# Power table stored and mask read back through ScalarE's own queue, first weights issued ahead of the mask

## The chip, the core and the metric

The kernel runs on one core of a Trainium2 chip. The metric is the device time of one execution in microseconds (us), the median of three runs. Engines are named as the profile names them: PE (TensorE), with PEld for its weight loads, DVE (VectorE), ACT (ScalarE), POOL (GpSimd) and SP (SyncE, which in this kernel does nothing but issue transfers).

## The reference: retention, a gated mixture, a feed-forward layer

Only the first of the three stages touches the change. It is a retention layer over 2 batches, 8 heads, 768 positions and 64 features, in blocks:

```
Dmask = np.where(rel >= 0, lam[:, None, None] ** rel[None, :, :], 0.0)
intra = np.einsum('bhic,bhjc->bhij', qb, kb) * Dmask[None]
intra = np.einsum('bhij,bhjd->bhid', intra, vb)
inter = np.einsum('bhid,bhde->bhie', qb * lam_pow[None], kv_state)
out[:, :, sl] = intra + inter
kv_state = lam_block[None, :, None, None] * kv_state + np.einsum('bhsd,bhse->bhde', kb_dec, vb)
```

Its output, 1536 tokens of 512 features, goes through four experts, `out += p[:, e:e + 1] * (relu(x @ w1[e]) @ w2[e])` with normalised gates `p`, and then through `(g @ w_out)` with `g = h * sigmoid(h)` and `h = x @ w_in`. These two stages are nearly all of the matrix work.

## The kernel before

**Tiling.** Retention works on blocks of 128 positions: 6 blocks (c) for each of 2 batches (b) make 12 units, u = 2c + b. A unit has four pieces: `prep` (`qs`, the queries times powers, POOL), `scores` (`ks` on POOL, `s` on PE, then `a` = `s` times `dmask` on DVE), `mix` (`xps` on PE, then its high and low parts `xhi` on ACT and `xlo` on DVE) and `carry` (`sps` on PE, then the state). Every large product is made of three products of a high and a low part. So a weight tile is split before use: ACT rounds it to the high part (`ua` from the raw tile `u`, `dh` from `d`, line 139), and DVE or POOL subtracts to get the low part (`ub`, `dl`, line 140). The raw tiles `u` (line 113) and `d` (line 118) have two buffers each, and the next load into one is issued after the split of the old content.

**Order.** The program fixes the order on each engine by the order in which it is written (a manual schedule). The experts' products (`ph`, line 469, then `po`, line 524) for the first 256 tokens begin once units 0 and 1 are mixed; the rest of the retention is put between them. `keep_warm` issues products on PE whose result nobody reads: three before the first scores, five between the scores and `xps`.

**Powers.** `powers()` loads `lam` (8 numbers), doubles its way to a table of 256 powers per head on DVE (`z`, line 268), stores it to memory (`zd`), and reads it back twice: as the mask `dmask` (two transfers of 256 KB, made of runs of 128 numbers with overlapping addresses) and as the factors `qdec` (two of 128 KB). Each of these, like every other transfer of the kernel before, is issued by SP. SP takes its instructions in order; one that waits holds up those behind it.

**Semaphores of transfers.** The framework gives transfers eight completion semaphores, DMAHW0 to DMAHW7, in turn. A transfer that takes a semaphore again is not issued until the transfer that used it last has landed. So SP also waits for transfers with whose data it has nothing to do. The listings below show these waits in brackets.

**Gates.** After the fourth step of the experts, `gates()` normalises the expert probabilities with nine small operations on DVE (lines 313 to 319, tile `gate`, loaded at line 309).

Of the kernel before, what the change touches and what calls it, by code (L numbers as in the profile page):

```python
# [37 lines left out]
def kernel(  # L38
# [10 lines left out]
    nc = tc.nc  # L49
# [25 lines left out]
    zd = dram.tile([H, 2 * P], F32, name="zd")  # L75
# [20 lines left out]
    def load_qk(c, b):  # L96
        t = ald.tile([P, 2, NPAIR, P], F32, tag="qk", name="qkt")
        nc.sync.dma_start(out=t, in_=qk[c, b])
        qk_t[c, b] = t

    def load_kv(c, b, parts=(slice(0, 2),)):
        if (c, b) not in kv_t:
            kv_t[c, b] = ald.tile([P, 2, H, D], F32, tag="kv", name="kvt")
        for j in parts:
            nc.sync.dma_start(out=kv_t[c, b][:, j], in_=kv[c, b, :, j])
# [25 lines left out]
    def load(j, n=1):  # L131
        for _ in range(n):
            if nxt[j] < len(seq):
                ph, i, src = seq[nxt[j]]
                nxt[j] += 1
                (load_up, load_down)[j](src, i, (ph, i))
# [120 lines left out]
    def powers():  # L257
        z = acst.tile([H, 2 * P], F32, name="z")
        nc.sync.dma_start(out=z[:, P:P + 1], in_=lam)
        nc.vector.memset(z[:, :P - 1], 0.0)  # L260
        nc.vector.memset(z[:, P - 1:P], 1.0)
        for b in range(B):
            load_qk(0, b)
        load_kv(0, 0, [1])
        m = 1
        while m < P:
            o = P - 1 + m
            nc.vector.tensor_scalar_mul(z[:, o + 1:o + 1 + m], z[:, P:o + 1], z[:, o:o + 1])
            m *= 2
        nc.sync.dma_start(out=zd, in_=z)  # L270
        load_kv(0, 1, [1])
        for m in range(2):
            nc.sync.dma_start(
                out=dmask[:, 2 * m:2 * m + 2],
                in_=bass.AP(
                    zd.tensor, zd.offset + m * H * P, [[1, P], [2 * P, NPAIR], [1, P]]
                ),
            )
        load(0)
        for b in range(B):  # L280
            load_kv(0, b, [0])
        for t in range(2):
            nc.sync.dma_start(
                out=qdec[t * D:(t + 1) * D],
                in_=bass.AP(
                    zd.tensor, zd.offset + t * 2 * P + P, [[0, D], [4 * P, NPAIR], [1, P]]
                ),
            )
        for b in range(B):
            nc.gpsimd.memset(state[b], 0.0)  # L290
        keep_warm(3)

    def keep_warm(n):
        warm = psum.tile([P, NPAIR, P], F32, tag="po3", name="warm")
        for _ in range(n):
            nc.tensor.matmul(
                warm, lhsT=state[0][:, 0], rhs=state[0], start=True, stop=True
            )
# [499 lines left out]

    with tc.manual_schedule():
        powers()  # L800
        load(1)
        load(0)
# [232 lines left out]
```

## Time and profile before

| | |
|---|---|
| Median of 3 runs | 828.22 us (827.99 to 828.74) |
| Profiled execution | 826.95 us, of which the span of the trace is 825.2 us |
| PE busy | 811.7 us, 98% of the span |
| DVE, ACT, POOL busy | 535.1, 323.0, 456.6 us |
| Granted TensorE clock | 1.0 of full over the span's 40 slices, by the page |

The profiled execution is 1.27 us below the median of the runs. Times in rows count from the start of the span. A row of a timeline gives start, duration, engine, source line, operation, output and inputs; in brackets stands how long the engine was idle before it and what ended that.

### The profile page before, as it was taken

What the parts mean: (1) busy time and instruction counts of PE and PEld (TensorE: products, weight loads), DVE (VectorE), ACT (ScalarE), POOL (GpSimd) and SP (SyncE); (2) the same over time, 40 slices, a digit from 0 to 9 for tenths busy, and PEclk for the clock granted to TensorE, in tenths of its full rate; (3) what the DMA queues carried; (4) which work ended last, traced back from release to release, by engine and by line L of the source; (5) the groups of instructions that cost most, each with busy time, mean ns of one, the idle gap of its engine ahead of it and who ended that gap; (6) DMA issues with size and microseconds to landing.
All of it is one profiled execution on the core that took longest, in us unless ns stands there. A gap on an engine that the chain in (4) does not pass through costs nothing.

```text
span 825.2 us, 10886 instructions
## 1 busy us (share of the span) xinstructions
PE 811.7 (98%) x4144; PEld 672.4 (81%) x4144; DVE 535.1 (65%) x776; ACT 323.0 (39%) x508; POOL 456.6 (55%) x334
## 2 busy tenths in 40 slices
PE   9899999999999999999999999999999999999998
PEld 5799778888878888888888888888888888888886
DVE  4876957475758577777877777765345345666666
ACT  3424232323346433333333333334445465444431
POOL 1724646353558566666666666654356566656631
PEclk9999999999999999999999999999999999999999
DMA  8885756542333223222322211222333131111002
GB/s 285 321 297 174 260 196 241 186 137 89 128 124 120 90 90 116 89 90 90 115 90 90 90 64 65 64 69 87 100 102 100 55 102 51 52 52 52 25 1 102
DMA packets 31432, 95.92 MB, mean 116 GB/s; under 512 B 3408, under 2 KB 5000, under 8 KB 31380
## 3 DMA queue, kind: packets, MB, share of 16 engines
q1 hardware_dynamic: 31380, 95.23, 34.4%
q8 instruction: 32, 0.52, 0.3%
q14 instruction: 20, 0.16, 0.1%
HBM read 83.65 MB, written 11.57 MB: 115 GB/s over the span
## 4 chain that ended last, share of the span: by engine, by line
PE 90%; DVE 5%; DMA 2%; ACT 1%; issue 1%; SPq 0%; ACTq 0%; DVEq 0%
PE po L706 32%; PE po L524 14%; PE ph L469 13%; PE y L646 12%; PE z L646 8%; PE x L646 8%; DMA d<-wts 2%; PE s L364 1%; PE xps L391 1%; PE xps L382 1%; DVE lo L562 1%; DVE tail L204 1%; DVE dec L207 1%; ACT hhi L496 0%; DVE dec L201 0%
## 5 line engine op out<-in xcount | busy, mean ns | idle before, releaser
L718 DVE TENSOR_TENSOR acc<-po,acc 128x512 f32<-128x512 f32 x176 | 117.2, 683 | 54.4 <-PE po L706 54.3
L706 PE MATMUL po<-hhi,dh 128*128 128x512 f32 x384 | 149.4, 389 | 0.0
L706 PE MATMUL po<-hhi,dl 128*128 128x512 f32 x384 | 149.4, 389 | 0.0
L706 PE MATMUL po<-hlo,dh 128*128 128x512 f32 x384 | 149.4, 389 | 0.0
L140 POOL TENSOR_TENSOR dl<-d,dh 128x1024 fp32r<-128x1024 f32 (+1 forms) x48 | 114.1, 2376 | 27.7 <-ACT dh L139 27.6
L140 POOL TENSOR_TENSOR ub<-u,ua 128x256 fp32r<-128x256 f32 (+2 forms) x48 | 75.5, 1573 | 91.8 <-ACT ua L139 87.5
L663 POOL TENSOR_TENSOR s<-s,s 128x512 f32<-128x512 f32 x48 | 68.5, 1428 | 45.0 <-ACT s L658 44.9
L140 POOL TENSOR_TENSOR uc<-u,uc 128x512 fp32r<-128x512 f32 x24 | 30.9, 1288 | 98.3 <-ACT uc L139 98.3
L706 PEld LDWEIGHTS po<-hhi,dl 128*128 128x128 f32 x384 | 72.1, 188 | 15.1
L706 PEld LDWEIGHTS po<-hlo,dh 128*128 128x128 f32 x384 | 72.1, 188 | 15.0
L706 PEld LDWEIGHTS po<-hhi,dh 128*128 128x128 f32 x384 | 72.1, 188 | 14.9
L496 ACT ACTIVATE hhi<-ph 128x512 fp32r<-128x512 f32 x40 | 24.0, 599 | 111.3 <-DVE ph L490 97.5
L140 POOL TENSOR_TENSOR ub<-us,ua 128x1024 fp32r<-128x1024 f32 x24 | 57.7, 2403 | 5.0 <-ACT ua L139 5.0
L469 PE MATMUL ph<-xhi,ua 128*128 128x512 f32 (+1 forms) x224 | 55.5, 370 | 3.5 <-DVE hlo L480 2.8
L524 PE MATMUL po<-hhi,dh 128*128 128x512 f32 (+1 forms) x224 | 58.7, 364 | 0.1
L524 PE MATMUL po<-hhi,dl 128*128 128x512 f32 (+1 forms) x224 | 57.7, 359 | 0.0
L524 PE MATMUL po<-hlo,dh 128*128 128x512 f32 (+1 forms) x224 | 57.6, 359 | 0.0
L139 ACT ACTIVATE dh<-d 128x1024 fp32r<-128x1024 f32 (+1 forms) x52 | 51.3, 988 | 11.3 <-issue 3.1
L469 PE MATMUL ph<-xhi,ub 128*128 128x512 f32 (+1 forms) x224 | 53.2, 359 | 0.0
L469 PE MATMUL ph<-xlo,ua 128*128 128x512 f32 (+1 forms) x224 | 53.0, 359 | 0.0
L343 POOL TENSOR_TENSOR qs<-qkt,qdec 128x512 f32<-128x512 f32 x10 | 12.9, 1290 | 67.3 <-PE xps L382 52.3
L469 PEld LDWEIGHTS ph<-xhi,ua 128*128 128x128 f32 x224 | 37.8, 188 | 11.8 <-DVE hlo L480 3.2
(127 smaller groups left out, 1600.9 us busy)
## 6 DMA issues: line engine op xcount, KB each, us to landing
u<-wts SPq DMA_DIRECT2D x32, 512.0 KB, 3.5
d<-wts SPq DMA_DIRECT2D x32, 512.0 KB, 4.0
words<-wts SPq DMA_DIRECT2D x32, 512.0 KB, 6.0
wd<-dec SPq DMA_DIRECT2D x32, 256.0 KB, 4.1
u<-wd SPq DMA_DIRECT2D x16, 512.0 KB, 3.7
d<-wd SPq DMA_DIRECT2D x16, 512.0 KB, 3.8
qkt<-qk SPq DMA_DIRECT2D x12, 512.0 KB, 6.2
kvt<-kv SPq DMA_DIRECT2D x10, 512.0 KB, 5.0
```

The lines of the kernel that those rows point to most:

```text
L139: nc.scalar.activation(out=hi, in_=src, func=AF.Copy)
L140: eng.tensor_tensor(out=lo, in0=src, in1=hi.bitcast(F32), op=ALU.subtract)
L204: nc.vector.tensor_scalar(out=tail, in0=low, scalar1=2.0 ** -29, scalar2=None, op0=ALU.mult)
L207: nc.vector.scalar_tensor_tensor(out=f, in0=high, scalar=3, in1=f, op0=ALU.logical_shift_left, op1=ALU.bitwise_or,)
L343: nc.gpsimd.tensor_tensor(out=qs, in0=qkt[:, 0], in1=qdec, op=ALU.mult)
L469: nc.tensor.matmul(pt[:, :n], lhsT=w, rhs=x[:, k, o:o + n], start=(j == 0), stop=(j == len(ops) - 1),)
L496: nc.scalar.activation(out=hi, in_=pt, func=AF.Copy)
L524: nc.tensor.matmul(po_t[d][:, :n], lhsT=w[:, d * P:(d + 1) * P], rhs=h[:, :n], start=(begin and j == 0), stop=(last and j == 2),)
L646: nc.tensor.matmul(to, lhsT=a[:, k * P:(k + 1) * P], rhs=b[:, k], start=(first and j == 0), stop=(j == len(ops) - 1), skip_group_check=not ...
L663: nc.gpsimd.tensor_tensor(out=t, in0=a, in1=b, op=ALU.add)
L706: nc.tensor.matmul(po, lhsT=w, rhs=h, start=(j == 0), stop=(j == len(ops) - 1))
L718: nc.vector.tensor_tensor(out=a, in0=po, in1=a, op=ALU.add)
```

## The change

In `powers()` the store of the table and the four reads of it (two of `dmask`, two of `qdec`) are issued by ACT in place of SP. The first load of up-weights, `load(0)`, is written ahead of the mask reads. Nothing else in the program is altered.

```
-        nc.sync.dma_start(out=zd, in_=z)
+
+        nc.scalar.dma_start(out=zd, in_=z)
         load_kv(0, 1, [1])
+        load(0)
         for m in range(2):
-            nc.sync.dma_start(
+            nc.scalar.dma_start(
                 out=dmask[:, 2 * m:2 * m + 2],
...
-        load(0)
         for b in range(B):
             load_kv(0, b, [0])
         for t in range(2):
-            nc.sync.dma_start(
+            nc.scalar.dma_start(
                 out=qdec[t * D:(t + 1) * D],
```

SP before, from the second half of the first values and keys to the third down-weight load. `zd` is the table in memory, `u` and `d` raw weights, `kvt` keys and values, `qkt` queries and keys; the two rows behind these are the `qkt` loads of block 1.

```order
L270 DMA zd<-z 8x256 [waits DMAHW0_49,DVE_49]
L105 DMA kvt<-kv 128x512
L273 DMA dmask<-zd 128x4x128 [waits DMAHW4_49]
L273 DMA dmask<-zd 128x4x128
L113 DMA u_145<-wts 128x1024
L105 DMA kvt<-kv 128x512 [waits DMAHW1_49]
L105 DMA kvt<-kv 128x512 [waits DMAHW2_49]
L283 DMA qdec<-zd 64x4x128 [waits DMAHW3_49]
L283 DMA qdec<-zd 64x4x128
L118 DMA d_157<-wts 128x1024 [waits DMAHW5_49]
L113 DMA u_159<-wts 128x1024 [waits DMAHW6_49]
L118 DMA d_161<-wts 128x1024 [waits DMAHW7_49]
```

SP after, the same stretch, up to the `qkt` loads of block 1.

```order
L98 DMA qkt<-qk 128x1024 x2
L105 DMA kvt<-kv 128x512 x2
L113 DMA u_143<-wts 128x1024
L105 DMA kvt<-kv 128x512 [waits DMAHW0_49]
L105 DMA kvt<-kv 128x512 [waits DMAHW2_49]
L118 DMA d_157<-wts 128x1024 [waits DMAHW4_49]
L113 DMA u_159<-wts 128x1024 [waits DMAHW6_49]
L118 DMA d_161<-wts 128x1024 [waits DMAHW7_49]
L98 DMA qkt<-qk 128x1024 [waits DMAHW1_49,DMAHW0_49,PE_49]
L98 DMA qkt<-qk 128x1024 [waits DMAHW1_49,PE_49]
```

SP no longer waits for DVE or for the store before the first weights, but semaphores now tie its loads to ACT's transfers: the first `d` takes over DMAHW4 from the store, the second `u` takes DMAHW6 from the first `u`, the second `d` takes DMAHW7 from the first mask read, and the second `qkt` takes DMAHW1 from the second mask read.

ACT before, from its first instruction.

```order
L139 ACT_TABLE_LOAD
L139 ACTIVATE ua<-u_145 128x2x256 [waits DMAHW0_49]
L403 ACTIVATE xhi<-xps 128x4x128 [waits PE_49] x2
L139 ACTIVATE ua<-u_145 128x512
L139 ACTIVATE dh<-d_157 128x512 [waits DMAHW5_49]
```

ACT after, from its first instruction.

```order
L271 DMA zd<-z 8x256 [waits DMAHW0_49,DVE_49]
L275 DMA dmask<-zd 128x4x128 [waits DMAHW4_49]
L275 DMA dmask<-zd 128x4x128 [waits DMAHW1_49]
L284 DMA qdec<-zd 64x4x128 [waits DMAHW3_49]
L284 DMA qdec<-zd 64x4x128 [waits DMAHW5_49]
L139 ACT_TABLE_LOAD
L139 ACTIVATE ua<-u_143 128x2x256 [waits DMAHW6_49]
L404 ACTIVATE xhi<-xps 128x4x128 [waits PE_49] x2
```

The five transfers stand ahead of everything else on ACT, the load of its function table included. On PE, DVE and POOL the order of instructions is the same in both programs.

## Rows read from the trace of the kernel before

**Rows 1.** The page's first part: busy time, share, instructions.

```profile
PE 811.7 (98%) x4144; PEld 672.4 (81%) x4144; DVE 535.1 (65%) x776; ACT 323.0 (39%) x508; POOL 456.6 (55%) x334
```

**Rows 2.** Longest wait of PE in the whole span: total us, times, longest.

```profile
PE ph L469 <- DVE hlo L480: 2.8, 1, 2.8
```

**Rows 3.** Windows: length, busy PE PEld DVE ACT POOL, clock, DMA share, GB/s.

```profile
36.19:38.98 2.79, 0.00 (x1) 0.00 (x1) 2.79 (x5) 0.00 (x0) 2.71 (x4) 1.00 1.01 389
60.00:825.00 765.00, 756.64 (x3659) 626.37 (x3658) 493.93 (x695) 304.13 (x472) 432.76 (x308) 1.00 0.31 102
```

**Rows 4.** The chain that ended last, at 4 us: start, duration, what.

```profile
4.02 2.75 DMA zd<-z
```

**Rows 5.** Timeline of PE, 8 to 16 us.

```profile
8.60 4.56 PE L296 MATMUL warm<-state 128*128 128x512 f32 x10
13.09 1.97 PE L391 MATMUL xps<-a,kvt 128*64 128x128 f32 x32
15.76 0.51 PE L469 MATMUL ph<-xhi,ua 128*128 128x256 f32 x2 [0.70 <-ACT xhi L403]
```

**Rows 6.** Timeline of DVE and ACT, 8 to 16 us.

```profile
10.69 2.78 DVE L372 TENSOR_TENSOR a<-s,dmask 128x256 f32<-128x256 f32 x8 [6.69 <-DMA dmask<-zd]
13.07 0.63 ACT L139 ACTIVATE ua<-u 128x512 fp32r<-128x512 f32 x1 [11.05 <-DMA u<-wts]
15.11 0.60 ACT L403 ACTIVATE xhi<-xps 128x512 fp32r<-128x512 f32 x1 [0.28 <-PE xps L391]
```

**Rows 7.** Windows of the first 30 us, columns as in rows 3.

```profile
4.20:6.20 2.00, 2.00 (x4) 0.51 (x2) 0.00 (x0) 0.00 (x0) 0.00 (x0) 1.00 0.99 394
6.20:7.20 1.00, 1.00 (x11) 0.59 (x12) 0.00 (x0) 0.00 (x0) 0.00 (x0) 1.00 0.54 207
7.20:8.20 1.00, 1.00 (x24) 1.00 (x22) 0.00 (x0) 0.00 (x0) 0.00 (x0) 1.00 0.05 16
8.20:10.20 2.00, 2.00 (x14) 1.14 (x11) 0.00 (x0) 0.00 (x0) 0.00 (x0) 1.00 0.79 223
...
16.20:28.20 12.00, 11.98 (x126) 11.25 (x125) 7.58 (x16) 6.76 (x15) 4.36 (x5) 1.00 1.03 409
```

**Rows 8.** Timeline of PE, PEld, ACT and DVE, 23 to 29 us.

```profile
23.52 0.53 PEld L469 LDWEIGHTS ph<-xhi,ub 128*128 128x128 f32 x4 [0.21 <-DVE ub L140]
24.58 0.63 ACT L139 ACTIVATE ua<-u 128x512 fp32r<-128x512 f32 x1 [2.91 <-DMA u<-wts]
26.11 1.16 PE L364 MATMUL s<-qkt 64*128 64x128 f32 x16
27.27 0.54 PEld L469 LDWEIGHTS ph<-xhi,ua 128*128 128x128 f32 x4 [0.20 <-DVE hlo L480]
28.45 1.28 DVE L372 TENSOR_TENSOR a<-s,dmask 128x512 f32<-128x512 f32 x2
```

**Rows 9.** Tile `gate`, to 46 us: ns min/median/max, first and last start; landing.

```profile
L319 DVE TENSOR_TENSOR gate<-gate x4: 291/1020/1362, 35.1 to 37.9; 12x128 f32<-12x128 f32 x4
L309 SPq DMA_DIRECT2D gate<-probs x1: 390/390/390, 24.5 to 24.5; - x1
...
DMA to landing us min/median/max: 5.2/5.2/5.2
```

**Rows 10.** Timeline of ACT and SP, 0 to 8 us.

```profile
0.73 1.28 ACT L139 ACT_TABLE_LOAD   x1 [0.73 <-PEq L1022]
2.06 0.43 SPq L105 DMA_DIRECT2D kvt<-kv  x1
7.76 0.50 SPq L113 DMA_DIRECT2D u<-wts  x1
```

**Rows 11.** Tile `zd`: issues of its reads, ns; issue to landing of `dmask`.

```profile
L273 SPq DMA_DIRECT2D dmask<-zd x2: 382/445/508, 6.8 to 7.2; - x2
L283 SPq DMA_DIRECT2D qdec<-zd x2: 679/704/728, 9.4 to 10.2; - x2
...
DMA to landing us min/median/max: 3.8/4.0/4.2
```

## The prediction

> **What bounds the kernel now.** I read the busy shares first: PE works 811.7 of 825.2 us [rows 1], so no change of waits can win more than 13.5 us. PE's waits come next: the longest is 2.8 us, for DVE's `hlo`, and ends at 38.98 [rows 2, 3]; the stretch from 60 us on has another 765.0 − 756.6 = 8.4 us without PE work [rows 3], which no transfer of the start reaches directly.
>
> The chain of waits looks as if the start hung on the power table: it names 2.75 us for the store [rows 4], and DVE's first `a` waits 6.69 us for the mask [rows 6]. The reader should not take this for PE's path. PE fills that time with products nobody reads, until 13.16, and they stand ahead of `xps` in its order [rows 5]. So `xps` starts at 13.1 however early its inputs are. It ends at 15.06, the second `xhi` runs from 15.11 to 15.71 [rows 6], and `ph` starts at 15.76 [rows 5]. The first `ua` was done at 13.70 [rows 6]. So **weights that come earlier save nothing at the first `ph`**.
>
> Then the transfers, the full resource of the first 30 us. From 16.2 to 28.2 the DMA engines are busy at share 1.03 with 409 GB/s, but from 7.2 to 8.2 they stand nearly idle (0.05), while the mask waits for the store [rows 7]. What that backlog delays is seen at 24 to 30 us: ACT waits 2.91 us for the third `u`, and its later `hhi` and DVE's `hlo` follow late, so `a` of unit 2 starts at 28.45 [rows 8] and ends at 29.7. The gates come next on DVE, and the probabilities land just then, 24.5 + 5.2 = 29.7 [rows 9]. Nine gate operations stand ahead of the `hlo` for which PE waits at 38.98.
>
> **The change part by part.**
>
> *SP.* It loses a wait: the first `u` is issued at about 2.9 (one `kvt` issue at 2.06 takes 0.43, a second as much) in place of 7.76 [rows 10]. By the new order the first `d` waits only for the store. The second `d` and the second `qkt` wait for the two halves of the mask.
>
> *ACT.* It issues five transfers, by SP's durations 0.38 + 0.51 for the mask, 0.68 + 0.73 for `qdec` and, taken like the shortest of these, 0.38 for the store, 2.7 us [rows 11], waits for the store between, and loads its table behind them, 1.28 us [rows 10]. From 6.2 us, when I put the store's landing: 0.9 for the mask, 1.4 for `qdec`, 1.3 for the table, done at 9.8. I cost it at nothing: ACT has nothing before 13.07 now [rows 6], and PE needs from it the `xhi` behind `xps`. Without that cover it would cost the whole 3.6 us. No row has a transfer issued by ACT; were each issue twice as long, ACT would be free by 12.1.
>
> *The gain, behind the backlog.* Idle shares times lengths, 0.46 × 1 + 0.95 × 1 + 0.21 × 2 = 1.8 us between 6.2 and 10.2 [rows 7], can be filled with weights; and the mask moved at 223 GB/s where large rows moved at 394, so mixed with these it may give back some more. I take 2 us: the third `u`, its `d` and the probabilities land 2 us sooner. Then `a` of unit 2 hangs on PE's scores and no longer on ACT: these start at 26.11 less the PEld stall of 0.21, last 1.16 and end at 27.06, against the start of `a` at 28.45: **1.4 us** [rows 8]. Gates and `hlo` follow by as much. PE arrives 0.4 us sooner (0.21 and 0.20), so its stall of 2.79 shrinks to 1.8, and PE goes on 1.4 us ahead. Bounds: 0 if the stream gains nothing, 2.79 + 0.41 = 3.2 us if the whole stall goes.
>
> *The loss, at the mask.* Now the mask reads are alone in the one queue, ahead of the weights: issued at 6.8 and 7.2, they land 3.8 and 4.2 us later, at 10.6 and 11.4 [rows 11]. The first two of eight `a` start at 10.69; the other six need the second half and take from 11.40 to 13.47, 2.07 us [rows 6]. A quarter of `xps` (0.49) must follow the last `a`. So `xps` ends at T + 2.56, where T is the landing of the second half, and not before 15.06 [rows 5]: **up to T = 12.5 nothing is lost, from there each us late costs PE one**. After the change the mask shares the engines with whatever SP has out. Low bound: it is served at once; the store takes 2.75 us as today at most, T is 11.4 or less, loss 0. High bound: all that SP may have out goes first. From 2.4 to 7.6 us, at 394 GB/s, the queue moves 2 MB: two `qkt`, two `kvt` and `u` (a 128x1024 tile of 4-byte numbers is 512 KB). Left are two `kvt` of 256 KB, `d` and the second `u`, 1.57 MB or 4.0 us. With a store 0.6 us quicker than now, since it no longer stands behind `qkt` and `kvt`, T = 11.4 − 0.6 + 4.0 = 14.8, loss 2.3 us. I take T = 13.6, **loss 1.1 us**, the middle: the mask goes in runs of 512 bytes, `u` in rows of 4 KB, so by turns the mask has the worse of it, but `u` and the second `u` come one after the other.
>
> The Trainium skill (DMA: Bandwidth & Descriptors, "Queues, rings and completion order") says that each DMA engine goes round the queues that have work, a packet of several descriptors at a time. If such packets hold about the same time on both queues, T by that rule would be near 12.8 and the loss 0.3 us, an estimate. No run here has two queues at work yet.
>
> *Sum.* −1.4 + 1.1 = −0.3 us on the profiled 826.95, which lies 1.27 below the median: 826.65 there, **827.9 us** beside the median of 828.22.
>
> **The rivals.**
>
> *The mask is starved* (slower). If SP's second `d`, free once the first mask half has landed, also passes the second half, T rises by another 1.3 us to 16.1, the loss to 3.6, the sum to +2.2: 830.4 us. For it: large rows against short ones, and a second `d` that waits for the first half only. Against: `u`, `d` and the second `u` wait for semaphores and so come in slices. It decides from T = 12.5 + 1.4 + 1.66 = 15.6 on.
>
> *The mask is served at once.* Loss 0, sum −1.4: 826.8 us. For it: the store and mask then have a queue without a backlog. Against: the same 16 engines.
>
> *The whole stall goes* (faster). One gate operation took 291 ns against a median of 1020 [rows 9], while POOL worked through nearly all of the stall (2.71 of 2.79) [rows 3]. If POOL, fed earlier, is through with its splits, nine gates take some 2.6 us and not 9: sum −3.2, 825.0 us. Against: POOL's work follows ACT and PE, and it is busy to the end of the stall.
>
> *No gain from the order of issue.* The stream is full from 10 us on; if its semaphores hold SP up as long as the store did, `u` and probabilities come at today's times: 828.2, or 829.3 with the mask late. The Trainium skill (same page, "Issuing engines are not separate DMA queues") states just this: a second issuing engine saves sequencer time alone. The trace bears it out in part, since the stream runs at share 1.03, but it also shows the idle 2 us.
>
> **How the numbers follow.** Chances: forecast (mask late by 0 to 2.3 us beyond its slack, sum −1.4 to +0.9) 0.50; starved 0.16; served at once 0.17; whole stall 0.09; no gain 0.08. About 0.2% (1.66 us) is what a measurement of this kernel can tell from no change. Forecast and no gain lie within it but for 1 in 20 on either side, since the 8.4 us without PE work after 60 us [rows 3] may shift by about 1 us; so do four fifths of served at once; starved is slower in all but 1 of 10. Together faster 0.15, same 0.67, slower 0.18. The likeliest case spans 826.8 to 829.1; the range reaches to the starved case and below served at once: 826.3 to 830.2.
>
> **What would show it.** Right: the first `u` issued near 3 us; `a` of units 0 and 1 starting later than 10.69, with a gap between its first two and the rest; `xps` ending at 15.1 to 17.4; no wait of ACT for the third `u`; PE's stall at 36 us near 1.8. Wrong: `xps` after 17.4 (starved), DVE's gates much shorter than 9 us (whole stall), ACT still waiting some 2.9 us for the third `u` (no gain), or a change of PE's waits after 60 us larger than that before.

## The result, and the profile after

The changed kernel takes 833.92 us (median of 6 runs, 832.81 to 835.88) beside 828.61 us for the kernel before: ratio 1.006, 95% interval 1.0048 to 1.0072. It is 5.3 us slower, where 827.9 us and no change that can be told were forecast. The profiled execution has 832.96 us with a span of 831.2, 6.0 us more than the span before.

The timeline of the start, after. The lines stand in order of time; those of ACT's queue are marked ACTq, those of SP's SPq.

```profile
3.02 0.52 SPq L113 DMA_DIRECT2D u<-wts  x1
3.58 2.96 SPq L105 DMA_DIRECT2D kvt<-kv  x2
3.87 0.55 ACTq L271 DMA_DIRECT2D zd<-z  x1
7.68 4.56 PE L297 MATMUL warm<-state 128*128 128x512 f32 x10
9.70 0.33 SPq L118 DMA_DIRECT2D d<-wts  x1
9.70 0.99 ACTq L275 DMA_DIRECT2D dmask<-zd  x2
10.11 0.40 SPq L113 DMA_DIRECT2D u<-wts  x1
12.39 1.28 ACT L139 ACT_TABLE_LOAD   x1 [12.39 <-issue]
16.53 0.33 SPq L118 DMA_DIRECT2D d<-wts  x1
16.61 0.76 DVE L373 TENSOR_TENSOR a<-s,dmask 128x256 f32<-128x256 f32 x2 [12.77 <-DMA dmask<-zd]
17.83 2.08 DVE L373 TENSOR_TENSOR a<-s,dmask 128x256 f32<-128x256 f32 x6 [0.46 <-DMA dmask<-zd]
18.35 3.56 PE L392 MATMUL xps<-a,kvt 128*64 128x128 f32 x32 [6.11 <-issue]
22.62 0.73 PE L470 MATMUL ph<-xhi,ua 128*128 128x256 f32 x4 [0.70 <-ACT xhi L404]
...
37.00 0.44 DVE L314 TENSOR_TENSOR gate<-gate 12x128 f32<-12x128 f32 x1 [1.05 <-DMA gate<-probs]
```

What to see, against [rows 4 to 6]: the store is issued at 3.87, a little sooner than before, but the reads of it only at 9.70, where the wait for the store ends; before these were 4.02 and 6.79. The second half of the mask lets `a` go on at 17.83, before at 11.4. PE has emptied its warm products at 12.24 and stands idle for 6.11 us. Then `xps` takes 3.56 us, where it took 1.97. The first `ph` starts 22.62 − 15.76 = 6.86 us later than before.

That the store stood behind SP's transfers is seen in the packets by queue (q1 is SP's, q10 is ACT's and is not there in the kernel before; packets, MB, share of the 16 engines), first from 4.5 to 7.5 us, then from 7.5 to 9.5:

```profile
q1 hardware_dynamic: 431, 1.08, 98.9%
```

```profile
q1 hardware_dynamic: 302, 0.69, 95.7%
q10 hardware_dynamic: 16, 0.01, 1.4%
```

ACT had issued the store by 4.42, but no packet of it moved before 7.5 us, while SP's filled the engines.

Why `xps` is slower stands in the windows (columns as in [rows 3]; the three numbers at the end are the granted clock, the DMA share and GB/s).

```profile
10.00:11.00 1.00, 1.00 (x4) 0.50 (x3) 0.00 (x0) 0.00 (x0) 0.00 (x0) 1.00 0.27 68
...
14.00:15.00 1.00, 0.00 (x0) 0.00 (x0) 0.00 (x0) 0.31 (x1) 0.00 (x0) 0.92 1.04 406
15.00:16.00 1.00, 0.00 (x0) 0.00 (x0) 0.00 (x0) 0.00 (x0) 0.00 (x0) 0.50 1.07 347
...
20.00:21.00 1.00, 1.00 (x14) 1.00 (x12) 0.55 (x1) 0.60 (x1) 0.01 (x1) 0.50 0.90 315
21.00:22.00 1.00, 0.92 (x10) 0.63 (x6) 0.69 (x1) 0.03 (x1) 0.00 (x0) 0.67 0.88 352
```

PE idles from 12.24; late in the window from 14 to 15 the granted clock drops from 1.00 to 0.50, the lower level of 1.2 GHz, and stays there through `xps`, until after 21. The DMA engines are busy meanwhile, at a share of 1.04 and 1.07: the mask waits its turn. They were not from 10 to 11 us: SP's `d` waits for the store's landing too, so the stream ran low (0.27) just when the mask reads were issued.

The wait of PE that answers to [rows 2], after:

```profile
PE ph L470 <- DVE hlo L481: 1.6, 1, 1.6
```

The stall behind the gates has shrunk from 2.8 to 1.6 us, so part of the forecast gain is there: of the 6.86 us lost at the first `ph`, some 0.8 us come back by the end of that stall, and the span ends 6.0 us longer.

### The profile page after: what moved, and what is told of

It reads as the page before. It is cut to its first block, busy times and chain, and to the rows that moved or that the text cites. A ratio compares the mean times of both kernels' runs of the same rounds, so it can differ in the third digit from the quotient of the medians.

```text
span 831.2 us, 10886 instructions
## 1 busy us (share of the span) xinstructions
PE 812.2 (98%) x4144; PEld 673.9 (81%) x4144; DVE 533.8 (64%) x776; ACT 323.2 (39%) x508; POOL 456.8 (55%) x334
## 4 chain that ended last, share of the span: by engine, by line
PE 91%; DVE 5%; issue 1%; DMA 1%; ACT 1%; POOL 0%; SPq 0%; ACTq 0%; DVEq 0%; POOLq 0%
PE po L707 31%; PE po L525 14%; PE ph L470 13%; PE y L647 12%; PE z L647 8%; PE x L647 8%; PE xps L392 1%; PE s L365 1%; PE warm L297 1%; PE xps L383 1%; DMA wd<-dec 1%; DVE lo L563 1%; DMA gate<-probs 1%; DVE tail L204 1%; DVE dec L207 1%
```

## The experiments

Eight kernels were run. The theory that took shape from the trace above: **a queue of its own gives the store and the mask no precedence; they come behind whatever SP has issued before or beside them, and SP, no longer waiting, now issues more.** The first rival: it is the weights written ahead of the mask. The second: transfers issued by ACT are slow in themselves. Ratios are to the kernel before on the same chip, with the 95% interval.

### The two halves of the change, each alone

First, the weights ahead, all transfers with SP: the store, and likewise the four reads of mask and decays.

```
-        nc.scalar.dma_start(out=zd, in_=z)
+        nc.sync.dma_start(out=zd, in_=z)
...
         load_kv(0, 1, [1])
         load(0)
```

> Half of the change alone: all transfers stay with SP, only the first weight load is written ahead of the mask reads. Theory 'the own queue gives no precedence' (what SP issued ahead of the store and the mask is moved first, wherever they are queued): the store keeps its place behind 1.25 MB and lands near 6.8 us, the mask reads stand behind one more 512 KB load, so the second half lands near 12.0 to 12.7 and xps ends at 15.1 to 15.4; the transfers have no idle stretch at 7.2 to 8.2 us, so PE's stall at 36 us shrinks by about 1 us: 827.0 to 828.2 us, nothing lost. Rival 'weights ahead of the mask are what costs': the mask half lands after 15 us and most of the 5 us loss of the changed kernel is here.

Measured: 827.68 us, ratio 0.9987 (0.9977 to 0.9997), a gain of about 1 us. Its timeline:

```profile
6.65 0.93 SPq L275 DMA_DIRECT2D dmask<-zd  x2
10.16 0.63 ACT L139 ACTIVATE ua<-u 128x512 fp32r<-128x512 f32 x1 [8.14 <-DMA u<-wts]
11.36 2.87 DVE L373 TENSOR_TENSOR a<-s,dmask 128x256 f32<-128x256 f32 x8 [7.50 <-DMA dmask<-zd]
15.64 0.74 PE L470 MATMUL ph<-xhi,ua 128*128 128x256 f32 x4 [0.70 <-ACT xhi L404]
```

The mask is 0.7 us later than before, within its slack, and the first `ph` is not later at all. The first rival falls. The stall behind the gates is 2.4 us, only 0.4 us less than before, where about 1 us less was expected.

Then the queue alone, for the store and the four reads, with `load(0)` in its old place.

```
-        nc.sync.dma_start(out=zd, in_=z)
+        nc.scalar.dma_start(out=zd, in_=z)
```

> The other half alone: store, mask and qdec issued by ACT, the first weight load written where it was. SP has nothing left to wait for between, so the order on SP and on ACT comes out as in the changed kernel. Theory 'own queue gives no precedence': as the changed kernel, 833 to 835 us, the store landing near 9.7 and the second mask half near 17.8 us. Rival 'weights ahead of the mask are what costs': back near 828.6 us.

Measured: 834.52 us, ratio 1.0071 (1.0056 to 1.0087). Its reads are issued at 9.15 and its `a` goes on at 17.13:

```profile
9.15 0.99 ACTq L273 DMA_DIRECT2D dmask<-zd  x2
17.13 2.08 DVE L372 TENSOR_TENSOR a<-s,dmask 128x256 f32<-128x256 f32 x6 [0.23 <-DMA dmask<-zd]
```

The whole loss comes with ACT's queue; the weights ahead are by themselves a small gain (the run before). This run parts the two less well than it seems: with nothing of `powers()` left on SP, `u` is issued at 3.01 here too, so SP's and ACT's orders are those of the changed kernel.

### The store given back to SP

```
-        nc.scalar.dma_start(out=zd, in_=z)
+        nc.sync.dma_start(out=zd, in_=z)
```

> The changed kernel with the store alone given back to SP, where it stands ahead of the second kvt half, of u and of the other kvt loads. Theory 'own queue gives no precedence': the store lands near 6.8 us, the mask reads on ACT start some 3 us sooner than in the changed kernel but behind u, two kvt and beside d: second half at 13.5 to 15.5 us, xps ends at 16 to 18, 829 to 832 us. Rival 'transfers issued by ACT are slow in themselves': the mask still needs some 8 us from its issue, as in the changed kernel (9.70 to 17.83), so it lands near 15 or later, with few bytes of SP in flight beside it.

Measured: 831.83 us (830.98 to 834.55), ratio 1.0046 (1.0027 to 1.0064), in the theory's range. The profiled execution is the slowest of the five, 834.55. In it the mask came later than the theory's 13.5 to 15.5 us:

```profile
6.62 0.98 ACTq L275 DMA_DIRECT2D dmask<-zd  x2
9.96 0.33 SPq L113 DMA_DIRECT2D u<-wts  x1
16.66 2.08 DVE L373 TENSOR_TENSOR a<-s,dmask 128x256 f32<-128x256 f32 x6 [2.08 <-DMA dmask<-zd]
```

The reads are issued 3.1 us sooner than in the changed kernel, and the second half is in only 1.2 us sooner, 10.0 us after the issue. That fits a mask that waits also for the second `u`, issued 3.3 us behind it; taken alone it would fit the second rival as well. The next run parts them.

### ACT's queue without company

SP's later loads are held until the mask is in, by a store of 4 KB of its second half.

```
         load_kv(0, 1, [1])
-        load(0)
         for m in range(2):
             nc.scalar.dma_start(out=dmask[:, 2 * m:2 * m + 2], ...)
+        hold = dram.tile([8, P], F32, name="hold")
+        nc.sync.dma_start(out=hold, in_=dmask[:8, 3, 1])
+        load(0)
         for b in range(B):
             load_kv(0, b, [0])
```

> ACT issues store, mask and qdec as in the changed kernel, but SP first writes 4 KB of the second mask half back to memory and so issues u, the rest of kvt, d and the second u only once the mask is in. Theory 'the mask waits behind what SP has on the same engines': with only qkt and kvt ahead (1.5 MB) the store lands at 6.5 to 7.3 us and the mask halves 3.7 to 4.8 us after their issue, as when SP issued them, so a starts at 10.5 to 11.5; the weights are then later than before and the total is between the kernel before and the changed one. Rival 'transfers issued by ACT are slow in themselves': the mask halves still need 7 to 8 us from their issue, a starting at 13.5 us or later.

Measured: 833.12 us, ratio 1.0051 (1.0032 to 1.007), from two runs. What was asked of it is in the timeline:

```profile
3.87 0.55 ACTq L271 DMA_DIRECT2D zd<-z  x1
7.60 0.94 ACTq L274 DMA_DIRECT2D dmask<-zd  x2
11.52 0.76 DVE L375 TENSOR_TENSOR a<-s,dmask 128x256 f32<-128x256 f32 x2 [7.69 <-DMA dmask<-zd]
12.56 2.08 DVE L375 TENSOR_TENSOR a<-s,dmask 128x256 f32<-128x256 f32 x6 [0.28 <-DMA dmask<-zd]
...
17.28 0.63 ACT L139 ACTIVATE ua<-u 128x512 fp32r<-128x512 f32 x1 [6.07 <-DMA u<-wts]
18.94 0.76 PE L472 MATMUL ph<-xhi,ua 128*128 128x256 f32 x4 [3.59 <-ACT xhi L406]
```

The same reads, issued by the same engine, land 3.9 and 4.5 us after their issue when SP sends nothing beside them; issued by SP alone they took 3.8 and 4.2 [rows 11]. The second rival falls. The kernel is slower than the one before all the same, since the weights now come 4.2 us later and `ph` starts 3.2 us later, behind them; the clock also falls to 0.50 behind that wait. In these two kernels with two queues either the mask is late or the weights are.

Three kernels give one line. From the issue of the first mask read to the go of the last six `a` it takes 5.0 us with nothing beside it, 8.1 us in the changed kernel, where SP sent `d` and the second `u` (1.05 MB), and 10.0 us with the store on SP, where the first `u`, two `kvt`, `d` and the second `u` were out (2.1 MB). At 400 GB/s these bytes are 2.6 and 5.2 us; added to 5.0 they give 7.6 and 10.2. The store goes the same way: 2.8 us from its issue to the reads' issue with 1.25 MB ahead of it on SP [rows 4], 3.7 in the last run with 1.5 MB ahead, 5.8 in the changed kernel with 2.3 MB. Which of the bytes to count was settled only after these runs had been seen.

### How the two queues take turns: not settled

The mask is read in one transfer in place of two; a small read of `lam` stands in the place of the second.

```
-        for m in range(2):
-            nc.scalar.dma_start(out=dmask[:, 2 * m:2 * m + 2], ...)
+        nc.scalar.dma_start(out=dmask,
+            in_=bass.AP(zd.tensor, zd.offset, [[1, P], [2 * P, H], [1, P]]))
+        nc.scalar.dma_start(out=spare, in_=lam)
```

> The changed kernel with the mask read as one transfer of 512 KB in place of two of 256 KB (a 32-byte read of lam takes the second one's place in the order, so that SP waits for the same semaphores). Theory 'the two queues take turns by whole transfers': the mask needs one turn, behind the first d but ahead of the second u, and is all in near 16.2 us, 1.6 us sooner than the second half now (17.83); xps ends 1.0 to 1.8 us sooner, 832 to 833 us. Rival 'turns by single pieces, so that long rows always win': the whole mask lands when its second half did, 17.5 to 18 us, and the time stays at 833.5 to 834.5 us.

Measured: 834.86 us, ratio 1.0071 (1.0058 to 1.0085). The theory of turns by whole transfers missed:

```profile
9.23 0.44 ACTq L274 DMA_DIRECT2D dmask<-zd  x1
...
17.91 2.74 DVE L372 TENSOR_TENSOR a<-s,dmask 128x256 f32<-128x256 f32 x8 [14.06 <-DMA dmask<-zd]
```

The whole mask is in when the second half was before, as the rival said of the landing. But the packets by queue (as above) do not bear the rival out; from 12.5 to 14 us, and then from 14 to 15.5, they are:

```profile
q10 hardware_dynamic: 650, 0.33, 91.7%
q1 hardware_dynamic: 23, 0.05, 11.3%
```

```profile
q1 hardware_dynamic: 106, 0.43, 74.6%
q10 hardware_dynamic: 287, 0.14, 32.2%
```

The second `u`, issued at 9.86, had the longer rows, and yet most of the mask's 0.52 MB moved ahead of it; only the last part came in behind it, by 17.8 us. In the changed kernel the trace has 16 completions for each of these transfers: 15 of the first half's by 14.78 us, the second `u`'s from 15.45 to 16.43, the second half's from 16.24 to 17.81. So there the queues did take turns by whole transfers, but for one part of the first half, which came at 16.52; and a half counts as landed only with its last part. Why the mask in one was split in two by `u`, and why that one part came late, stays open.

### What the clock is worth

Six more warm products keep PE busy until the mask is in.

```
-        keep_warm(5)
+        keep_warm(11)
```

> The changed kernel with 11 in place of 5 warm products ahead of xps, so that PE works nearly up to the mask's landing (5.5 us more, to 17.7 us, of its 6.1 us idle). In the changed kernel the granted clock was 0.62 from 13.2 to 20.0 us and xps took 3.6 us against 2.0 before. Theory 'part of the loss is the clock': xps takes 2.0 us again, 1.4 to 1.8 us less than the changed kernel, near 832.2 us. Rival 'the clock costs nothing, only the mask does': 833.9 us or more.

Measured: 834.67 us (830.99 to 835.06), ratio 1.0063 (1.0039 to 1.0087): no gain on the changed kernel in the median. The profiled execution is the slowest of the four, 835.06. In its timeline and windows (of PE: length, busy, clock, DMA share, GB/s):

```profile
18.26 2.18 PE L392 MATMUL xps<-a,kvt 128*64 128x128 f32 x32
21.14 0.74 PE L470 MATMUL ph<-xhi,ua 128*128 128x256 f32 x4 [0.70 <-ACT xhi L404]
```

```profile
44.00:45.00 1.00, 1.00 (x6) 0.51 0.96 344
45.00:46.00 1.00, 1.00 (x7) 0.50 0.98 344
46.00:47.00 1.00, 1.00 (x7) 0.50 0.97 357
47.00:48.00 1.00, 1.00 (x16) 0.78 0.81 327
...
113.00:114.00 1.00, 1.00 (x3) 0.50 0.83 236
```

The step itself came out as expected: `xps` takes 2.2 us again and the first `ph` is 1.5 us sooner. It is lost at the next stall. PE waits 2.0 us behind the gates, and with its return the clock is at 0.50 for more than 3 us; the sum over these windows is 0.49 + 0.50 + 0.50 + 0.22 = 1.7 us. A second spell from 112 to 116 us, behind a wait of PE of 1.3 us, costs as much again (0.35 + 0.50 + 0.50 + 0.35). In the profiled run of the changed kernel the stall of 1.6 us had no such spell behind it. One of the four runs kept a mean clock of 1.0 and took 830.99 us; the others had 0.995 or 0.996. So the step at `xps` is worth what was expected, but most runs lose it again at later stalls.

### Towards a better kernel: the gates

The run with the weights ahead on SP shows the same spell behind PE's stall of 2.4 us (windows of PE: length, busy, clock, DMA):

```profile
38.00:39.00 1.00, 0.60 (x5) 1.00 0.79 311
39.00:40.00 1.00, 1.00 (x9) 0.68 0.75 291
40.00:41.00 1.00, 1.00 (x7) 0.50 0.98 377
```

So that stall costs twice, and what makes it are nine gate operations that could be done at 4 to 10 us, where DVE and POOL are idle. On top of the weights ahead (the two calls at their old places, among the experts' steps, are taken out):

```
         load_kv(0, 0, [1])
+        load_probs()
...
         nc.sync.dma_start(out=zd, in_=z)
+        gates()
```

> All transfers on SP with the first weights ahead of the mask (827.7 us), and the gates taken out of DVE's way: their probabilities loaded before the store, the nine operations done on DVE between the power table and the mask, where DVE and POOL have nothing to do. Theory 'the 2.4 us stall of PE near 37 us is the gates, and in most runs a spell of 3.4 us at the lower granted clock follows it': gate operations take 0.2 to 0.3 us each (2 to 3 us in all), the stall is 0 to 0.5 us, no spell follows it, 823.5 to 825.5 us. Rival 'POOL and the weights set that stall, whoever stands ahead of hlo on DVE': PE still waits 1.5 us or more near 37 us and the time stays above 826.5 us.

Measured: 826.26 us, ratio 0.997 (0.9957 to 0.9983): faster than both kernels, by 2.3 us against the one before, though less than the 823.5 to 825.5 that were expected.

```profile
7.00 0.28 DVE L316 TENSOR_TENSOR gate<-gate 12x128 f32<-12x128 f32 x1 [3.15 <-DMA gate<-probs]
...
9.17 0.89 DVE L322 TENSOR_TENSOR gate<-gate 12x128 f32<-12x128 f32 x4
11.68 2.93 DVE L375 TENSOR_TENSOR a<-s,dmask 128x256 f32<-128x256 f32 x8 [1.63 <-DMA dmask<-zd]
13.06 2.26 PE L394 MATMUL xps<-a,kvt 128*64 128x128 f32 x32 [0.79 <-issue]
```

The nine operations take 3.1 us from 7.00 on, the stall near 37 us is gone (PE is busy without a break from 35 to 40 us), and in half of the runs the mean clock is 1.0. But the mask is later by another 0.3 us, and PE now waits for it, 0.8 us at `xps`. Was it then right to leave the weights ahead of the mask? The gates moved alone, in the kernel before:

> The kernel before with the gates moved alone (probabilities loaded before the store, nine gate operations ahead of the mask product), all transfers in their old order. In the run before, with the first weights ahead of the mask, 'a' started at 11.68 in place of 10.69 us and xps waited 0.8 us. Theory 'with the gates out of the way the start is bound by the mask, so weights ahead of it now cost': xps does not wait, ph starts near 15.8, the stall near 37 us is gone, 825.0 to 826.2 us, at or under the 826.26 of the run before. Rival 'weights ahead of the mask still pay, because the transfers are the bound of the first 30 us': ACT waits longer for the third u and d, PE stalls 1 to 2 us behind them, 826.6 to 828 us.

Measured: 828.62 us (825.77 to 830.94), ratio 0.9985 (0.9972 to 0.9997). Neither side came out: the median lies above both ranges. As the theory said, `xps` does not wait and `ph` starts at 15.45; as the rival said, ACT waits for weights (2.04 us for the first `d`), but PE stops for only 0.5 us, at 20 us.

```profile
17.96 1.15 ACT L139 ACTIVATE dh<-d 128x512 fp32r<-128x512 f32 x2 [2.04 <-DMA d<-wts]
20.40 0.71 PE L471 MATMUL ph<-xhi,ua 128*128 128x256 f32 x4 [0.55 <-DVE hlo L482]
```

The profiled execution took 826.54 us: five of the twelve runs have a mean clock of 0.999 or 1.0 and take 825.77 to 826.93, seven have 0.997 or 0.998 and take 828.59 or more. The point estimates say that the weights ahead still pay, by about 1 us; but the two ratios come from different chips and their intervals meet, so that is not shown.

## Why the prediction was wrong

**The slack, and the slope behind it: right.** PE's own warm products hide the mask up to T = 12.5 us, and each later microsecond costs one. T was 17.83, which is 5.3 us past the slack. The first `ph` came 6.86 us later; the other 1.6 us are `xps` at the lower clock (3.56 against 1.97).

**The step that failed: T, from the store on.** The sum had "a store 0.6 us quicker than now, since it no longer stands behind `qkt` and `kvt`". It was 3.0 us slower: 5.8 us from its issue to the reads' issue, against 2.8. The premise was false: `qkt` and `kvt` were still ahead of it, on the other queue, and the packets show that it did not pass them. The engine that issues a transfer did not take it out of the stream. By freeing SP from its waits the change put 1 MB ahead of the store, the first `u` and two `kvt` halves, which before had stood behind it. The high bound of 14.8 let SP's stream run full to 7.6 us and counted everything that SP might have out, but set all of it ahead of the mask and none ahead of the store, whose landing it put at 6.2. The reads were issued at 9.70, and to its 5.0 us alone came 2.6 us for `d` and the second `u`, some 0.5 us short of what was measured. So T lay 4.2 us past the value taken, 3.5 of it the store's, and 3.0 past the high bound.

**The rule that was weighed.** The rule on turns between queues (the Trainium skill, DMA: Bandwidth & Descriptors, "Queues, rings and completion order") would have let an 8 KB store through after a packet or so of SP's. The store on ACT took 3.7 us with 1.5 MB issued before it on the other queue and 5.8 with 2.3 MB, and in the changed kernel its first packet moved 3.2 us after its issue had ended: that does not bear the rule out. The mask did take turns with `d` and the second `u`, but by whole transfers, so T came nowhere near the 12.8 of that estimate. The Trainium skill (same page, "Issuing engines are not separate DMA queues") says that transfers of all issuing engines run on the same 16 DMA engines, and that a second one saves sequencer time alone. The trace agrees: in the run with the mask in one transfer the two queues' shares of the engines add up to 103% from 12.5 to 14 us and to 107% from 14 to 15.5, and nothing was sped up. It stood under the rival "no gain", where it was read as harmless.

**The clock: left out.** The prediction had no term for what PE's idle time does to the clock, although it named the case of a late mask. The lower level cost 1.6 us at `xps` in the profiled run, and the six runs have mean clocks of 0.992 to 0.996. It also took the profiled 826.95 us, 1.27 below the median, as an offset without a cause; the clock may be that cause. In the kernel before the stall at 36.19 to 38.98 was followed by no spell in the profiled run, but its 14 runs beside the first experiments all had mean clocks of 0.995 to 0.998; 0.2% of 828 us is 1.7 us, what one spell costs in the profiles that have one. Where it sits in those runs is not shown: the profiles of the other kernels have spells near 40 us, at 112 and at 245 us.

**The gain: right in kind, 0.8 in place of 1.4 us.** The stall fell to 1.6 us, and ACT's wait for the third `u` from 2.91 to 0.85. But the gates did not start with the end of `a`: DVE waited 1.05 us more for the probabilities. These had landed in time for it before, and were now issued at 31.8 in place of 24.5 us, 7.3 later, while the first `ph` was 6.86 later. Without the late mask, in the kernel with the weights ahead, the whole was worth about 1 us.

**ACT's issues: free, as costed.** ACT was through with its table at 13.67 and not at 9.8, but its first `xhi` was due only at 20.4.

**The rivals.** "The mask is starved" had the sign and the place right (`xps` ended at 21.9, past 17.4), but not the mechanism. It wanted SP's second `d` to pass the second half of the mask; that `d` was issued at 16.53 and landed from 19.33 on, after the mask. What made the mask late was the late store, and then `d` and the second `u`; its 830.4 us fell 3.5 us short, by the store and by the clock. That its sign was right is partly luck.

## What to carry to other kernels

Moving a transfer to another issuing engine moves its waits, not its place: before doing it, add up the bytes that the freed engine will now issue ahead of it. What should land first must be issued first, and best in the same queue: in the kernel before, `u` and two `kvt` were issued right behind the mask on SP, and its halves still landed 3.8 and 4.2 us after their issue [rows 10, 11]. Keeping the loads back by a wait is no cure by itself: with SP held, the mask was in time and the weights were late. A stall of PE may cost twice, since in several profiles the clock fell when it ended; the mean clock of the runs tells whether the profiled one is typical.

## What was not expected of the hardware

A transfer of 8 KB, on ACT's queue, took 5.8 us until its completion was seen with 2.3 MB issued before it on SP's, and 3.7 us with 1.5 MB; on SP's own queue it took 2.8 us with 1.25 MB ahead. Gate operations of 12x128 took 0.28 us at 7 us with the gates early, POOL idle, and 1.25 us in the changed kernel at 37 us, with POOL at work. And PE's return from 2.0 to 2.4 us of idling near 40 us found the clock at 0.50 for about 3.4 us in four profiles (weights ahead on SP, store on SP, six more warm products, SP held), and its return from 2.3 us at 243 us did so in two (queue alone, mask in one). After 2.8 us (the kernel before) and after 1.6 and 2.3 us (the changed kernel) it did not fall. What decides it is not shown.
